# Laying the scratch copy of P out as one run of rows per batch, and issuing its transfers from SP

## The chip, the cores and the metric

The kernel runs on one core of a Trainium2 chip. The metric is the device time of one execution in microseconds (us). All numbers below are of one core, and "the profile" is one profiled execution of the kernel.

## What is computed

Eight batches of cross attention between 512 tokens `x` and 32 states per head feed one gated layer. The output is `(A * B) @ w_out`, with `A` and `B` the attention output times `w_a` and `w_b`.

```python
scores = scale * x @ state.T            # per batch (8) and head (8): 512 x 32
xread  = softmax(scores) @ state        # 512 x 64
scores2 = scale * state @ x.T
sread  = softmax(scores2) @ x           # 32 x 64
attn = concatenate([xread, sread], axis=2)   # 544 tokens a batch
X = attn.transpose(0, 2, 1, 3).reshape(8 * 544, 512)
out = (X @ w_a * (X @ w_b)) @ w_out     # w_a, w_b: 512 x 1536; w_out: 1536 x 512
```

The inputs are float32, and the products are made of high and low halves (`_h`, `_l`).

## The kernel before

`xread` is never formed. Since `xread @ w` is `softmax(scores) @ (state @ w)`, the kernel first makes P, the product of every head's states with that head's 64 rows of the weights, and then multiplies the attention weights `at_h`, `at_l` with P. The 1536 columns are taken in six chunks `c` of two column tiles `ft`. A head pair is `hp` (0 to 3), half a batch's heads are a group `g`, and four batches are a batch group `bg`.

- `load_w` and `conv_w` fetch a chunk's weights (64-bit words, `raw<-wl`, issued by SP) and split them on ACT and DVE into `wq`.
- `project` (L141 to L145) multiplies the split states `sd_h`, `sd_l` of four batches with `wq`. ACT copies the result from PSUM into `sw_st`, a tile with two buffers, once for each head `hh` of the pair, and after the second copy a transfer writes it to the scratch tensor `scr` in DRAM. In `scr` a batch's rows stand apart for each head.
- `Batch.load` (L269) reads one batch's part of P back into `p_raw` (two buffers), one transfer for each group `g`. All transfers into and out of `scr` are issued by ACT.
- `split` (L279, L65) turns `p_raw` into `p_h` and `p_l`, on ACT and on DVE or POOL. Four of the pieces are made by `direct` (L290 to L293) without `scr`.
- `layer1` (L379 to L387) multiplies P with the attention weights, and makes the gated product `g_h`, `g_l`. `layer2` (L402), two steps later, adds the output product into `acc`. Sums of a batch that is taken up again are kept in DRAM (`part`, L306 and L323).
- The attention itself (`x_raw`, `x_nat`, `s_p`, `at_h`, L178 to L240) and the last unit for the states' own tokens are spread among the steps.

The work is written as a list of 108 steps. A table (`VISITS`) gives the order of batches and chunks, and others give the step of each conversion. All projections and all first uses of P lie in the first half. A scheduler sets, when the kernel is built, one fixed order of instructions on each engine, and each engine then works through its own list, waiting where the next instruction's inputs or buffers aren't ready. Each transfer's completion is told through one of eight counters (`DMAHW0` to `DMAHW7`) that transfers of ACT and SP take in turn; a transfer that takes a counter again waits for the one before it on that counter.

Of the kernel before, what the change touches and what calls it, by code (L numbers as in the profile page):

```python
# [8 lines left out]
F32 = mybir.dt.float32  # L9
F32R = mybir.dt.float32r  # L10
# [6 lines left out]
B, H, S, NS, D = 8, 8, 512, 32, 64  # L17
DM, DFF = 512, 1536
P = 128
TOK = S + NS  # L20
NG = 2
NFT = DFF // P
NC = NFT // 2
# [25 lines left out]
def attn_moe(ctx, tc, xt, xn, sd, wl, w_out, out):  # L49
    nc = tc.nc  # L50

    const = ctx.enter_context(tc.tile_pool(name="const", bufs=1))
    proj = ctx.enter_context(tc.tile_pool(name="proj", bufs=2))
    att = ctx.enter_context(tc.tile_pool(name="att", bufs=2))
    mlp = ctx.enter_context(tc.tile_pool(name="mlp", bufs=2))
    dram = ctx.enter_context(tc.tile_pool(name="dram", bufs=1, space=bass.MemoryType.DRAM))
# [4 lines left out]
    def f32(ap):  # L61
        return ap.bitcast(F32)

    def minus(eng, out, in0, in1):
        eng.tensor_tensor(out=out, in0=in0, in1=in1, op=ALU.subtract)  # L65
# [40 lines left out]


    LO, HI, ALL = slice(0, D), slice(D, P), slice(0, P)
    sd_h = [proj.tile([P, 4, B * NS], F32R, name=f"sd_h{j}", bufs=1) for j in range(2)]
    sd_l = [proj.tile([P, 4, B * NS], F32R, name=f"sd_l{j}", bufs=1) for j in range(2)]  # L110

    def states():
        for j in range(2):
            raw = mlp.tile([P, 4, B * NS], F32, name="p_raw")
            nc.scalar.dma_start(out=raw, in_=sd[:, 4 * j:4 * j + 4])
            nc.scalar.copy(out=sd_h[j], in_=raw)
            minus(nc.gpsimd, sd_l[j], raw, f32(sd_h[j]))


    scr = [[dram.tile([H, 4 * NS, 512], F32, name=f"scr{c}_{g}") for g in range(2)] for c in range(NC)]  # L120
    w = {}

    def load_w(c, hp, place):
# [11 lines left out]
    def project(c, hp, bg, hh, psp, tag):  # L135
        if hh == 0:
            st[bg] = proj.tile([P, 2, 512], F32, name="sw_st")
        sw = st[bg]
        ps = psp.tile([P, 512], F32, name=tag)
        for k, s in enumerate((sd_h, sd_l)):  # L140
            nc.tensor.matmul(ps, lhsT=s[hp // 2][:, 2 * (hp % 2) + hh, bg * P:(bg + 1) * P], rhs=w[c, hp][:, hh],  # L141
                             start=(k == 0), stop=(k == 1))
        nc.scalar.copy(out=sw[:, hh], in_=ps)  # L143
        if hh:
            nc.scalar.dma_start(out=scr[c][bg][2 * hp:2 * hp + 2].rearrange("h n x -> n h x"), in_=sw)  # L145


    xst = const.tile([P, 4, B, NS], F32, name="xst")
# [15 lines left out]
    class Attention:  # L164
# [5 lines left out]
        def load(self):  # L170
            self.x = att.tile([P, 2, S + D], F32, name="x_raw", bufs=1)
            nc.sync.dma_start(out=self.x, in_=xt[self.b, self.g])
# [85 lines left out]
    class Batch:  # L258
        n, nk = S, NG
# [4 lines left out]

        def load(self, c):
            raw = self.raw[c] = mlp.tile([P, NG, 512], F32, name="p_raw")
            b = self.b
            for g in range(NG):
                nc.scalar.dma_start(out=raw[:, g],  # L269
                                    in_=scr[c][b // 4][4 * g:4 * g + 4, b % 4 * NS:(b % 4 + 1) * NS])  # L270

        def new_piece(self, c):
            self.pieces[c] = tuple(mlp.tile([P, NG, 512], F32R, name=n) for n in ("p_h", "p_l"))
# [8 lines left out]
        def direct(self, c, g):  # L282

            if g == 0:
                self.new_piece(c)
            ps = ps_ms.tile([P, 512], F32, name="ms")
            n = slice(self.b * NS, (self.b + 1) * NS)
            for i, s in enumerate((sd_h, sd_l)):
                for hq in range(4):
                    nc.tensor.matmul(ps[hq * NS:(hq + 1) * NS], lhsT=f32(s[g][:, hq, n]),  # L290
                                     rhs=f32(w[c, 2 * g + hq // 2][:, hq % 2]), start=(i == 0), stop=(i == 1))
            ph, pl = self.pieces[c]
            nc.scalar.copy(out=ph[:, g], in_=ps)  # L293
            minus(nc.vector, pl[:, g], ps, f32(ph[:, g]))
# [32 lines left out]
    class States:  # L327
        n, nk, begun = B * NS, 4, False
        pieces, raw = {}, {}
# [40 lines left out]
    def layer1(u, ft):  # L370
        res = []
        for ab in range(2):
            ps = ps_ab.tile([P, 512], F32, name="ab")
            m = 0
            for k in range(u.nk):
                xh, xl = u.rhs(k)
                wh, wlo = u.lhs(ft, k, ab)
                for a, b in ((wh, xh), (wh, xl), (wlo, xh)):
                    nc.tensor.matmul(ps[:, :u.n], lhsT=a, rhs=b, start=(m == 0), stop=(m == 3 * u.nk - 1))  # L379
                    m += 1  # L380
            res.append(ps)
        g = mlp.tile([P, 512], F32, name="a_sb")[:, :u.n]
        nc.scalar.copy(out=g, in_=res[0][:, :u.n])  # L383
        nc.vector.tensor_tensor(out=g, in0=res[1][:, :u.n], in1=g, op=ALU.mult)  # L384
        gh = mlp.tile([P, 512], F32R, name="g_h", bufs=LAG + 1)[:, :u.n]
        gl = mlp.tile([P, 512], F32R, name="g_l", bufs=LAG + 1)[:, :u.n]
        nc.scalar.copy(out=gh, in_=g)  # L387
        minus(nc.vector, gl, g, f32(gh))
        return gh, gl
# [31 lines left out]
    def mms(where, n, c, hp, bg):  # L421
        for hh in range(2):
            at(where, n, project, c, hp, bg, hh, *((ps_acc, "acc") if n < 0 else (ps_ms, "ms")))
# [28 lines left out]
    def conv0(hp):  # L452
# [3 lines left out]
    a0, a1, a2 = [[atts[b, g] for g in range(2)] for b in range(3)]  # L456
    done[0] = -1
    begin += [a0[0].load, next_load, states, lambda: new_a(0),
              lambda: conv0(0), a0[0].scores, a0[0].soft, a0[1].load, lambda: conv0(1), a0[0].norm,
              a0[1].scores, a0[0].nat, lambda: units[0].direct(0, 0), a0[0].back]  # L460
# [39 lines left out]
    for v, (u, cs) in enumerate(VISITS):  # L500
        s = starts[v]
# [7 lines left out]
        for i, c in enumerate(cs):  # L509
            n = s + 2 * i  # L510
# [5 lines left out]
            t = max(n - 6, (CONV[c][3] + 1 if c else 0) + u // 4)  # L516
# [9 lines left out]
    for n, (u, ft, first, last, final) in enumerate(steps):  # L526
        for f in front[n]:
            f()
        g = layer1(u, ft)
# [50 lines left out]
```

## Time and profile before

| | |
|---|---|
| median of 3 runs | 810.42 us (809.29 to 811.74) |
| profiled execution: its time, its span | 809.78 us, 807.9 us |
| busy in the span: PE, DVE, ACT, POOL | 736.5, 504.7, 372.5, 130.1 us |
| mean granted TensorE clock | 0.966 |
| transfers of P: stores of 512 KB, loads of 256 KB | 48, 88 |

PE (TensorE) is the busiest engine. Busy times are sums over the whole run, and the first 450 us are another regime than the rest: projections, conversions and attention run beside the two layers there. A row of the chain view reads: start, length, what the last-ended work was then doing or waiting for. A row of the timeline has the start, the length, the engine, line, operation and tiles, and, in brackets, how long the engine sat idle before it and what ended that. ACTq and SPq are the engines' queues of transfer issues. PEld is the loading of weights, which overlaps PE.

### The profile page before, as it was taken

Reading aid. Unit: us, or ns where it says so; the run is one execution under the profiler, and the core shown is the slowest. Engines: PE = TensorE matmul, PEld = TensorE weight load, DVE = VectorE, ACT = ScalarE, POOL = GpSimd, SP = SyncE. Lnnn points to the kernel's source line nnn. Section 1 sums busy time; section 2 is a strip of 40 time slices with the busy share of each in tenths; the row PEclk is TensorE's granted clock in tenths of the full one; section 3 lists DMA queues with packets and bytes.
Section 4 is the critical chain, followed back from the end, with each engine's and each line's share of the span. In section 5 each row is a group of like instructions: output and inputs, shape, how many; then the busy total and the mean of one; then the engine's idle time right before and its main releaser. Section 6 shows DMA issues by size and latency. Waiting matters only on the chain.

```text
span 807.9 us, 9570 instructions
## 1 busy us (share of the span) xinstructions
PE 736.5 (91%) x3384; PEld 555.2 (69%) x3384; DVE 504.7 (62%) x885; ACT 372.5 (46%) x686; POOL 130.1 (16%) x100
## 2 busy tenths in 40 slices
PE   1668879898998999998889999999999999999997
PEld 0345545573765768886667677777788888888886
DVE  5977851866996675685269573654435953596422
ACT  4546644735654455665444333343334633453222
POOL 3213110001222031010022241322110010100100
PEclk9989779999998999999999999999999999999999
DMA  8567854586366536556657772413013521241002
GB/s 315 194 232 264 285 189 156 174 295 239 125 229 230 197 139 240 193 183 222 232 199 255 236 236 77 148 39 130 30 51 101 188 75 53 66 145 52 1 1 79
DMA packets 52560, 131.17 MB, mean 162 GB/s; under 512 B 3872, under 2 KB 3872, under 8 KB 52512
## 3 DMA queue, kind: packets, MB, share of 16 engines
q1 hardware_dynamic: 27552, 81.28, 29.7%
q10 hardware_dynamic: 24960, 49.29, 17.0%
q8 instruction: 26, 0.43, 0.2%
q14 instruction: 22, 0.18, 0.1%
HBM read 84.93 MB, written 45.61 MB: 162 GB/s over the span
## 4 chain that ended last, share of the span: by engine, by line
PE 64%; DMA 15%; DVE 12%; ACT 5%; issue 2%; ACTq 1%; POOL 0%; DVEq 0%; POOLq 0%
PE ab L379 29%; PE acc L402 27%; DMA scr<-sw_st 8%; DMA p_raw<-scr 4%; PE ms L141 3%; PE ms L231 2%; DMA x_nat<-xn 2%; DVE t L92 1%; DVE wq L104 1%; DVE t L99 1%; DVE t L97 1%; ACT sw_st L143 1%; PE ms L178 1%; DMA raw<-wl 1%; PE ms L290 1%
## 5 line engine op out<-in xcount | busy, mean ns | idle before, releaser
L402 PE MATMUL acc<-wo,g_h 128*128 128x512 f32 x816 | 240.7, 399 | 4.3 <-DVE stg L318 4.3
L402 PEld LDWEIGHTS acc<-wo,g_h 128*128 128x128 f32 x816 | 153.3, 190 | 42.6 <-DVE stg L318 6.8
L384 DVE TENSOR_TENSOR a_sb<-ab,a_sb 128x512 f32<-128x512 f32 (+1 forms) x108 | 71.1, 658 | 173.6 <-PE ab L379 137.9
L379 PE MATMUL ab<-at_h,p_h 128*128 128x512 f32 x384 | 158.8, 416 | 11.3 <-ACT a_sb L383 7.3
L379 PE MATMUL ab<-at_h,p_l 128*128 128x512 f32 x384 | 153.4, 403 | 3.5 <-DVE p_l L65 3.5
L379 PE MATMUL ab<-at_l,p_h 128*128 128x512 f32 x384 | 154.8, 403 | 0.9 <-POOL at_l L65 0.9
L402 PE MATMUL acc<-wo,g_l 128*128 128x512 f32 x408 | 143.2, 399 | 0.0
L65 POOL TENSOR_TENSOR p_l<-p_raw,p_h 128x512 fp32r<-128x512 f32 x44 | 65.0, 1477 | 428.5 <-ACT p_h L279 385.9
L65 DVE TENSOR_TENSOR g_l<-a_sb,g_h 128x512 fp32r<-128x512 f32 (+1 forms) x108 | 91.0, 843 | 32.8 <-ACT g_h L387 31.0
L383 ACT COPY a_sb<-ab 128x512 f32<-128x512 f32 (+1 forms) x108 | 60.7, 562 | 101.6 <-PE ab L379 92.7
L387 ACT CAST g_h<-a_sb 128x512 fp32r<-128x512 f32 (+1 forms) x108 | 64.4, 596 | 86.9 <-DVE a_sb L384 86.3
L379 PEld LDWEIGHTS ab<-at_h,p_h 128*128 128x128 f32 x384 | 73.5, 193 | 39.7 <-ACT a_sb L383 10.3
L402 PEld LDWEIGHTS acc<-wo,g_l 128*128 128x128 f32 x408 | 77.4, 190 | 19.8 <-DVE g_l L65 1.0
L379 PEld LDWEIGHTS ab<-at_h,p_l 128*128 128x128 f32 x384 | 73.8, 193 | 23.1 <-DVE p_l L65 4.4
L379 PEld LDWEIGHTS ab<-at_l,p_h 128*128 128x128 f32 x384 | 74.4, 194 | 18.9 <-POOL at_l L65 2.2
L143 ACT COPY sw_st<-ms 128x512 f32<-128x512 f32 x88 | 50.8, 587 | 57.2 <-PE ms L141 22.1
L279 ACT CAST p_h<-p_raw 128x512 fp32r<-128x512 f32 x88 | 50.8, 619 | 49.9 <-PE ab L379 31.4
L141 PE MATMUL ms<-wq,sd_h 128*128 128x512 f32 x88 | 37.9, 431 | 10.3 <-ACT sw_st L143 9.5
L90 DVE TENSOR_SCALAR t<-t 128x512 int32<-128x512 int32 x60 | 28.2, 472 | 28.1 <-ACT t L89 27.6
L95 ACT CAST wq<-t 64x512 fp32r<-64x512 f32 (+1 forms) x64 | 39.4, 620 | 12.7 <-PE ms L290 4.9
L65 POOL TENSOR_TENSOR s_p<-s_p,m 128x512 f32<-128x512 f32 x16 | 18.3, 1146 | 113.1 <-DVE m L193 113.1
L141 PE MATMUL ms<-wq,sd_l 128*128 128x512 f32 x88 | 36.3, 413 | 0.0
(89 smaller groups left out, 816.2 us busy)
## 6 DMA issues: line engine op xcount, KB each, us to landing
scr<-sw_st ACTq DMA_DIRECT2D x48, 512.0 KB
p_raw<-scr ACTq DMA_DIRECT2D x88, 256.0 KB
raw<-wl SPq DMA_DIRECT2D x23, 512.0 KB
x_raw<-xt SPq DMA_DIRECT2D x16, 576.0 KB
part<-stg SPq DMA_DIRECT2D x18, 512.0 KB
stg<-part SPq DMA_DIRECT2D x18, 512.0 KB
out<-stg SPq DMA_DIRECT2D x34, 256.0 KB
x_nat<-xn SPq DMA_DIRECT2D x16, 512.0 KB
```

The costliest lines, as they stand in the source:

```text
L65: eng.tensor_tensor(out=out, in0=in0, in1=in1, op=ALU.subtract)
L90: nc.vector.tensor_scalar(out=t2, in0=t1, scalar1=3, scalar2=0x7FFFF000, op0=ALU.logical_shift_left, op1=ALU.bitwise_and)
L95: nc.scalar.copy(out=o, in_=f32(t2[rows]))
L141: nc.tensor.matmul(ps, lhsT=s[hp // 2][:, 2 * (hp % 2) + hh, bg * P:(bg + 1) * P], rhs=w[c, hp][:, hh], start=(k == 0), stop=(k == 1))
L143: nc.scalar.copy(out=sw[:, hh], in_=ps)
L231: nc.tensor.matmul(ps[hp * D:(hp + 1) * D, :P], lhsT=self.a2[:, sb, hp * D:(hp + 1) * D], rhs=self.xn[:, sb, hp * P:(hp + 1) * P], start=( ...
L279: nc.scalar.copy(out=ph[:, g], in_=self.raw[c][:, g])
L379: nc.tensor.matmul(ps[:, :u.n], lhsT=a, rhs=b, start=(m == 0), stop=(m == 3 * u.nk - 1))
L383: nc.scalar.copy(out=g, in_=res[0][:, :u.n])
L384: nc.vector.tensor_tensor(out=g, in0=res[1][:, :u.n], in1=g, op=ALU.mult)
L387: nc.scalar.copy(out=gh, in_=g)
L402: nc.tensor.matmul(u.acc[i], lhsT=l[:, ts], rhs=wo[ft][:, r], start=(first and k == 0), stop=(last and k == 2))
```

## The change

`scr` gets the shape group, batch of four, head of four, state, so that one batch's 128 rows of a group stand in one run. To let a store keep whole rows, the states' columns in `sd_h` and `sd_l` are put in the order state, batch (`states`, which now makes four copies of half the size with a reordering access), so that the projection's output rows come out in that order too. A store of 512 KB becomes two of 256 KB, one for each head. A load of both groups becomes one transfer of 512 KB. Both are issued by SP (`nc.sync`) instead of ACT (`nc.scalar`). `direct` reads its 32 columns of the states with a step of four.

```diff
-    sd_h = [proj.tile([P, 4, B * NS], F32R, name=f"sd_h{j}", bufs=1) for j in range(2)]
+    sd_h = [proj.tile([P, 4, 2, P], F32R, name=f"sd_h{j}", bufs=1) for j in range(2)]
...
-            nc.scalar.copy(out=sd_h[j], in_=raw)
-            minus(nc.gpsimd, sd_l[j], raw, f32(sd_h[j]))
+            for bg in range(2):
+                h, l = (t[j][:, :, bg].rearrange("p h (n b) -> p h b n", b=4) for t in (sd_h, sd_l))
+                r = raw[:, :, bg * P:(bg + 1) * P].rearrange("p h (b n) -> p h b n", b=4)
+                nc.scalar.copy(out=h, in_=r)
+                minus(nc.gpsimd, l, r, f32(h))
...
-    scr = [[dram.tile([H, 4 * NS, 512], F32, name=f"scr{c}_{g}") for g in range(2)] for c in range(NC)]
+    scr = [[dram.tile([NG, 4, 4, NS, 512], F32, name=f"scr{c}_{g}") for g in range(2)] for c in range(NC)]
...
         if hh:
-            nc.scalar.dma_start(out=scr[c][bg][2 * hp:2 * hp + 2].rearrange("h n x -> n h x"), in_=sw)
+            h = 2 * (hp % 2)
+            for i in range(2):
+                nc.sync.dma_start(out=scr[c][bg][hp // 2, :, h + i].rearrange("b n x -> n b x"), in_=sw[:, i])
...
-            for g in range(NG):
-                nc.scalar.dma_start(out=raw[:, g],
-                                    in_=scr[c][b // 4][4 * g:4 * g + 4, b % 4 * NS:(b % 4 + 1) * NS])
+            nc.sync.dma_start(out=raw, in_=scr[c][self.b // 4][:, self.b % 4].rearrange("g h n x -> (h n) g x"))
...
-                    nc.tensor.matmul(ps[hq * NS:(hq + 1) * NS], lhsT=f32(s[g][:, hq, n]),
+                    nc.tensor.matmul(ps[hq * NS:(hq + 1) * NS], lhsT=f32(s[g][:, hq, self.b // 4, self.b % 4::4]),
```

The orders below are those fixed when the kernels are built; lines are each kernel's own (L143 before is L148 after, L145 is L152, L269 is L274). The first place is ACT in the third chunk's projections, about 168 to 178 us into the profile of before. Before:

```order
L387 CAST g_h<-a_sb 128x512 [waits DVE_49]
L269 DMA p_raw<-scr_0_91 128x1x512 [waits DMAHW7_49,DMAHW4_49]
L269 DMA p_raw<-scr_0_91 128x1x512 [waits DMAHW0_49,Pool_49]
L143 COPY sw_st<-ms 128x512 [waits PE_49]
L383 COPY a_sb<-ab 128x512 [waits PE_49]
L145 DMA scr_1_92<-sw_st 128x2x512 [waits DMAHW1_49,Activation_49]
L143 COPY sw_st<-ms 128x512 [waits PE_49]
L387 CAST g_h<-a_sb 128x512 [waits DVE_49]
```

and after, on ACT at the same place:

```order
L390 CAST g_h<-a_sb 128x512 [waits DVE_49]
L148 COPY sw_st<-ms 128x512 [waits PE_49]
L148 COPY sw_st<-ms 128x512 [waits DMAHW1_49,DMAHW4_49,PE_49,Activation_49]
L386 COPY a_sb<-ab 128x512 [waits PE_49]
L390 CAST g_h<-a_sb 128x512 [waits DVE_49]
```

The loads and the store are gone from ACT's list. What stays is the copy's own wait for the buffer, now for two counters, since a buffer is left by two stores.

The second place is SP where the fifth chunk ends and the sixth begins, about 330 to 375 us. Before, SP has only weights there:

```order
L78 DMA raw<-wl 128x2x512 [waits DMAHW7_49,DVE_49]
L78 DMA raw<-w_out 128x1024 [waits DMAHW3_49,DVE_49,Activation_49]
L78 DMA raw<-w_out 128x1024 [waits DMAHW3_49,DMAHW5_49,DVE_49,Activation_49]
L78 DMA raw<-wl 128x1024 [waits DMAHW7_49,DVE_49]
L78 DMA raw<-wl 128x1024 [waits DMAHW1_49,DMAHW5_49,DVE_49,Activation_49]
```

and after, a part of the same stretch:

```order
L152 DMA scr_1_96<-sw_st 32x4x512 [waits DMAHW5_49,Activation_49]
L78 DMA raw<-w_out 128x1024 [waits DMAHW6_49,DMAHW2_49,DVE_49]
L152 DMA scr_1_96<-sw_st 32x4x512 [waits DMAHW7_49,Activation_49]
L78 DMA raw<-wl 128x1024 [waits DMAHW0_49,DVE_49]
L274 DMA p_raw<-scr_1_96 128x2x512 [waits DMAHW5_49,DMAHW7_49,DMAHW1_49,Pool_49]
L152 DMA scr_0_97<-sw_st 32x4x512 [waits Activation_49]
L152 DMA scr_0_97<-sw_st 32x4x512 [waits DMAHW3_49,Activation_49]
L78 DMA raw<-wl 128x1024 [waits DMAHW6_49,DMAHW4_49,DVE_49]
L152 DMA scr_1_98<-sw_st 32x4x512 [waits Activation_49]
L274 DMA p_raw<-scr_0_95 128x2x512 [waits DMAHW1_49,DVE_49,Pool_49]
```

The two halves of a store stand between loads of weights that wait for DVE, and the load of a piece, which waits for its stores to land, stands ahead of the next chunk's stores.

More of the change, by code (lines that the diff above doesn't have):

```diff
@@ L108, in attn_moe @@
     LO, HI, ALL = slice(0, D), slice(D, P), slice(0, P)
-    sd_h = [proj.tile([P, 4, B * NS], F32R, name=f"sd_h{j}", bufs=1) for j in range(2)]
-    sd_l = [proj.tile([P, 4, B * NS], F32R, name=f"sd_l{j}", bufs=1) for j in range(2)]
+    sd_h = [proj.tile([P, 4, 2, P], F32R, name=f"sd_h{j}", bufs=1) for j in range(2)]
+    sd_l = [proj.tile([P, 4, 2, P], F32R, name=f"sd_l{j}", bufs=1) for j in range(2)]
     def states():
@@ L140, in project @@
         for k, s in enumerate((sd_h, sd_l)):
-            nc.tensor.matmul(ps, lhsT=s[hp // 2][:, 2 * (hp % 2) + hh, bg * P:(bg + 1) * P], rhs=w[c, hp][:, hh],
+            nc.tensor.matmul(ps, lhsT=s[hp // 2][:, 2 * (hp % 2) + hh, bg], rhs=w[c, hp][:, hh],
                              start=(k == 0), stop=(k == 1))
@@ L266, in load @@
             raw = self.raw[c] = mlp.tile([P, NG, 512], F32, name="p_raw")
-            b = self.b
-            for g in range(NG):
-                nc.scalar.dma_start(out=raw[:, g],
-                                    in_=scr[c][b // 4][4 * g:4 * g + 4, b % 4 * NS:(b % 4 + 1) * NS])
+            nc.sync.dma_start(out=raw, in_=scr[c][self.b // 4][:, self.b % 4].rearrange("g h n x -> (h n) g x"))
         def new_piece(self, c):
@@ L286, in direct @@
             ps = ps_ms.tile([P, 512], F32, name="ms")
-            n = slice(self.b * NS, (self.b + 1) * NS)
             for i, s in enumerate((sd_h, sd_l)):
                 for hq in range(4):
-                    nc.tensor.matmul(ps[hq * NS:(hq + 1) * NS], lhsT=f32(s[g][:, hq, n]),
+                    nc.tensor.matmul(ps[hq * NS:(hq + 1) * NS], lhsT=f32(s[g][:, hq, self.b // 4, self.b % 4::4]),
                                      rhs=f32(w[c, 2 * g + hq // 2][:, hq % 2]), start=(i == 0), stop=(i == 1))
```

## Prediction

> **What bounds the kernel now.** I read the page first, for the whole and for PE:
>
> ```profile
> span 807.9 us, 9570 instructions
> PE 736.5 (91%) x3384; PEld 555.2 (69%) x3384; DVE 504.7 (62%) x885; ACT 372.5 (46%) x686; POOL 130.1 (16%) x100
> PE ab L379 29%; PE acc L402 27%; DMA scr<-sw_st 8%; DMA p_raw<-scr 4%; PE ms L141 3%; PE ms L231 2%; DMA x_nat<-xn 2%; DVE t L92 1%; DVE wq L104 1%; DVE t L99 1%; DVE t L97 1%; ACT sw_st L143 1%; PE ms L178 1%; DMA raw<-wl 1%; PE ms L290 1%
> ```
>
> PE is busy 91% of the span, so 71 us of it are idle. In the chain of waits the transfers of P hold 8% and 4%, some 97 us. That is a ceiling and not a gain: behind a chain there is always a second one. To place it, the stages (busy us of each engine, then granted clock, DMA share, GB/s):
>
> ```profile
> 28.00:62.00 34.00, 25.44 (x126) 14.46 (x127) 29.39 (x60) 16.48 (x32) 7.02 (x7) 0.85 0.68 225
> 160.00:196.00 36.00, 31.71 (x130) 22.67 (x130) 22.59 (x42) 14.86 (x29) 1.48 (x1) 0.93 0.76 278
> 200.00:250.00 50.00, 46.25 (x223) 34.88 (x222) 48.57 (x89) 29.90 (x56) 13.93 (x11) 1.00 0.54 192
> 354.00:410.00 56.00, 48.41 (x199) 37.51 (x198) 25.18 (x39) 25.27 (x47) 4.53 (x4) 0.97 0.67 231
> 450.00:808.00 358.00, 353.14 (x1697) 285.16 (x1695) 191.17 (x319) 135.06 (x249) 53.92 (x38) 1.00 0.28 93
> ```
>
> From 450 us on PE is full and DMA is at 0.28: loads of P are hidden there, and I cost that stage at nothing. What the change can move lies in three stages, 28 to 62, 160 to 196 and 354 to 410 us. Between them, at 200 to 250, DVE is busy 48.57 of 50 us: time won ahead of it is in part waited out there. The pieces of the chain in these stages (start, length):
>
> ```profile
> 41.17 9.57 DMA scr<-sw_st
> 129.96 2.86 DMA scr<-sw_st
> 164.73 8.25 DMA scr<-sw_st
> 174.81 7.66 DMA scr<-sw_st
> 355.14 5.21 DMA p_raw<-scr
> 361.55 9.09 DMA scr<-sw_st
> 381.13 15.01 DMA scr<-sw_st
> 400.86 8.26 DMA p_raw<-scr
> ```
>
> The same 512 KB store takes 2.86 us when nothing is in its way, and 7.7 to 15 us here. Next, who sat idle for it: ACT, by all its waits and at six places, and then PE at the same places.
>
> ```profile
> ACT sw_st L143 <- DMA scr<-sw_st: 21.5, 8, 6.0
> ACT p_h L279 <- DMA p_raw<-scr: 18.4, 6, 7.0
> 51.98 0.59 ACT L383 COPY a_sb<-ab 128x512 f32<-128x512 f32 x1 [6.20 <-DMA p_raw<-scr]
> 174.19 0.59 ACT L143 COPY sw_st<-ms 128x512 f32<-128x512 f32 x1 [5.54 <-issue]
> 182.54 0.59 ACT L143 COPY sw_st<-ms 128x512 f32<-128x512 f32 x1 [5.41 <-DMA scr<-sw_st]
> 370.72 1.08 ACT L143 COPY sw_st<-ms 128x512 f32<-128x512 f32 x2 [4.49 <-DMA scr<-sw_st]
> 396.23 1.07 ACT L143 COPY sw_st<-ms 128x512 f32<-128x512 f32 x2 [6.04 <-DMA scr<-sw_st]
> 409.14 0.62 ACT L279 CAST p_h<-p_raw 128x512 fp32r<-128x512 f32 x1 [7.04 <-DMA p_raw<-scr]
> 52.62 0.80 PE L379 MATMUL ab<-at_h,p_h 128*128 128x512 f32 x1 [3.28 <-ACT a_sb L383]
> 183.18 0.51 PE L141 MATMUL ms<-wq,sd_h 128*128 128x512 f32 x1 [1.84 <-ACT sw_st L143]
> 194.49 0.50 PE L379 MATMUL ab<-at_h,p_h 128*128 128x512 f32 x1 [1.85 <-ACT p_h L293]
> 371.36 0.50 PE L141 MATMUL ms<-wq,sd_h 128*128 128x512 f32 x1 [3.19 <-ACT sw_st L143]
> 396.86 0.50 PE L141 MATMUL ms<-wq,sd_h 128*128 128x512 f32 x1 [2.45 <-ACT sw_st L143]
> 410.29 0.50 PE L379 MATMUL ab<-at_h,p_h 128*128 128x512 f32 x1 [2.23 <-ACT a_sb L383]
> ```
>
> Two kinds of stall show. At 51.98, at 174.19 and before 194.49 ACT had nothing of its own to wait for: a load of P in its list waited for a store to land, and everything behind the load stood. At the others a copy waits for its `sw_st` buffer, or a split for its load. PE loses less than ACT, 14.8 us in these six rows, because it has other matmuls queued.
>
> Last, the transfers themselves:
>
> ```profile
> DMA packets 52560, 131.17 MB, mean 162 GB/s; under 512 B 3872, under 2 KB 3872, under 8 KB 52512
> q10 hardware_dynamic: 24960, 49.29, 17.0%
> ```
>
> q10 is ACT's queue. Its data packets are rows: 88 x 128 + 48 x 256 + 2 x 128 (the states) = 23808. The other 1152 are the small ones that tell of completion. If the 48 stores and 2 loads of states leave 16 each, one for each DMA engine, that is 800, and 352 are left for 88 loads: 4 each. So a load of P runs on 4 of the 16 DMA engines, and on those four everything behind it waits.
>
> **The change, part by part.**
>
> Loads leave ACT (first kind of stall). All three waits move to SP, on which no engine's arithmetic waits. PE's idle time there is 3.28 and 1.85 us; at 174.19 it has other work. Gain 5.1 us; at the least 0, if the next input is as late as the issue was.
>
> Loads change shape. The Trainium skill, "DMA: Bandwidth & Descriptors", section "Why a DMA increments its semaphore by 16 and not by 1", says that a transfer runs on the largest number of engines up to 16 that divides the slowest dimension of both sides; by it the old loads, with 4 heads outermost, get 4, which the count bears out, and the new ones, with 128 rows, get 16. No run here shows the new load yet. From rows: it carries 512 KB like the store that took 2.86, against 5.21 for 256 KB now, so 2.9 to 5.2 us a piece, and I take 3.5, nearer the row of its size. The split at 409.14 waited 7.04 of a load's 8.26 us. With the load at 5 us amid its neighbours, the wait shrinks by 3.3, and PE's 2.23 by the same share, 1.0 us.
>
> Stores land sooner (second kind). Above the 2.86 of an unhindered store the rows at 174.81, 361.55 and 381.13 have 4.8, 6.2 and 12.1 us. Part of that is loads on four engines ahead of the store, part is plain traffic, since DMA shares of 0.67 and 0.76 remain whoever issues. I take half: 2.4, 3.1 and 6.0 off the waits of 5.41, 4.49 and 6.04, which leaves 3.0, 1.4 and 0 of them; in proportion PE's 1.84, 3.19 and 2.45 shrink by 0.8, 2.2 and 2.45. Gain 5.5 us, between 0 and 7.5.
>
> The clock. The three stages lost 0.15 x 34 + 0.07 x 36 + 0.03 x 56 = 9.3 us to a granted clock under 1. PE idling less may bring a third back: 3 us, between 0 and 5.
>
> Costs. `states` makes four copies in place of two, and `direct` reads columns with a step:
>
> ```profile
> L116 ACT CAST sd_h<-p_raw 128x1024 fp32r<-128x1024 f32 x2 | 2.1, 1040 | 3.6 <-DMA p_raw<-sd 3.6
> L290 PEld LDWEIGHTS ms<-wq,sd_l 128*32 128x32 f32 x64 | 2.2, 119 | 5.8 <-issue 5.8
> ```
>
> Two casts of half the size at the 0.62 of a 128x512 one (row 409.14) are 0.2 us longer than one of 1.04, twice, on ACT while DVE's conversions lead: 0.2 us taken, 0 to 1. The stepped columns might double a load of 119 ns; over 128 that is 15 us at most, beside matmuls that last longer, so 0 taken. The two issues per store cost SP, not a working engine, some 0.4 us. A first half of a piece can no longer be loaded before the other is stored, but no split of these stages waits on the first half alone for long: 0.
>
> SP's own waits are the serious cost, since P now stands behind them (waits of SP's queue: us, times, longest):
>
> ```profile
> SPq L78 <- DVE wq L104: 273.8, 29, 65.5
> SPq L306 <- DMA part<-stg: 22.5, 9, 4.7
> ```
>
> Today nothing urgent is behind them: weights come early, and sums have slack. After the change stores stand behind both. The second sort is 2.5 us each; about five have a store of P behind them, and a store that is late by that is mostly covered by the other `sw_st` buffer. I take 2 us, and leave the first sort to a rival.
>
> Sum: 5.1 + 1.0 + 5.5 + 3 - 0.2 - 2 = 12.4 us less than the profiled execution's 809.8 (span 807.9 and 1.9 around it). The median of 810.4 stands 0.6 above that execution, so 798.0; I forecast 797.
>
> **The rivals.**
>
> Slower: SP holds the stores back. A load of weights that waits for DVE now stands between the halves of a store. A mean wait of the first SP row is 273.8 / 29 = 9.4 us. A step of the two layers is 24 matmuls, 5.8 us:
>
> ```profile
> 482.46 2.99 PE ab L379 x12
> 485.45 2.80 PE acc L402 x12
> ```
>
> A step with a conversion makes two stores, one for each batch group, and there are two buffers, so a store that is late by 9.4 us stalls ACT's copy, and PE after it, by some 3.6 us. Three to four such places use up the gain of 12.4, six give 798 + 22 = 820, and one wait as long as the longest, 65.5 us, would do it alone: 813 to 835. For it: the new order on SP shows such neighbours for each chunk. Against it: the order follows when things are expected to be ready, and on ACT stores already stood behind waits of the same size. The point of decision is whether DVE frees `raw` later than ACT finishes the copy beside it.
>
> Same: the queue does not matter. The Trainium skill, same page, section "Issuing engines are not separate DMA queues", says that issuing from several engines only saves the time to issue. In this kernel that would mean the waits for landing bind whoever issues: SP waits for a store in place of ACT, the buffers come free no sooner, and the time is 808 to 812. The rows speak against it in part: ACT stood 6.20 and 5.54 us for an issue alone.
>
> Much faster: the chain is the right measure. If the five long stores in the chain rows (49.6 us) came down to 2.86 each, 35 us would be gained there alone: 770 to 778. Against it: DVE's 48.57 of 50 us, and PE's idle rows, 14.8 us against 66 in the eight chain rows.
>
> **How the numbers follow.** Forecast (785 to 807) 0.56; slower 0.24; same 0.12; much faster 0.08. The range leaves about one in ten on each side: 774 to 822. What a measurement can tell from no change is 0.3%, 2.4 us. Faster than that: 0.56 + 0.08 and a little of the others' edges, 0.65; within: 0.11; slower: 0.24.
>
> **What would show it.** Right: the small packets show 16 for every load in place of 4; ACT's waits for P (21.5 and 18.4) halve; the first kind of stall is absent from ACT; the store rows in the chain fall under 6 us; from 450 us on nothing changes but the start. Wrong: SP rows with stores of P behind `raw` loads, ACT's `sw_st` waits above 21.5 us, or PE idle as long for other inputs, DVE's above all.

## The result, and the profile after

The changed kernel takes 784.1 us (median of four runs, 781.05 to 787.78) against 810.77 us for the kernel before (809.29 to 811.74): a ratio of 0.9675, 95% interval 0.9625 to 0.9724. That is 26.7 us less, where 12.4 us less were worked out. The profiled execution took 785.89 us, with a span of 784.1 us. The head of the profile's page, with the lines on packets, on SP's and ACT's queues (q1, q10), on the chain and on the issues of P:

```profile
span 784.1 us, 9701 instructions
PE 724.5 (92%) x3384; PEld 550.3 (70%) x3384; DVE 509.8 (65%) x885; ACT 374.0 (48%) x688; POOL 133.2 (17%) x102
...
DMA packets 53681, 131.18 MB, mean 167 GB/s; under 512 B 4992, under 2 KB 4992, under 8 KB 53632
...
q1 hardware_dynamic: 53344, 129.52, 48.1%
q10 hardware_dynamic: 288, 1.05, 0.4%
...
PE ab L382 30%; PE acc L405 29%; PE ms L146 3%; DMA scr<-sw_st 3%; DVE wq L104 3%; DVE t L92 3%; DVE t L99 3%; DMA raw<-wl 2%; DVE t L97 2%; PE ms L238 1%; DMA raw<-w_out 1%; DMA p_raw<-scr 1%; DVE a_sb L387 1%; PE ms L185 1%; DVE t L90 1%
...
scr<-sw_st SPq DMA_DIRECT2D x96, 256.0 KB, 3.7
p_raw<-scr SPq DMA_DIRECT2D x44, 512.0 KB, 3.8
```

In the chain the transfers of P fell from 8% and 4% to 3% and 1%, and single lines of the conversions of weights on DVE (`t`, `wq`) are now, at 3% each, as large as the stores; together these conversions hold 12%. The small packets rose from 3872 to 4992: 48 more stores at 16 are 768, and 44 loads at 16 in place of 88 at 4 are 352 more. The sum is 1120, the whole difference, so a load of P now runs on 16 engines.

From the span and PE's busy time a split follows that the prediction did not make. Before, 736.5 us busy and 71.4 idle; after, 724.5 and 59.6. So 11.8 us are idle time saved, and 12.0 us are the same 3384 matmuls running shorter. The mean granted clocks agree: 0.966 of 807.9 us leaves 27.5 us without clock, 0.980 of 784.1 us leaves 15.7, which is 11.8 us less. The windows show where (busy us of each engine, then granted clock, DMA share, GB/s):

```profile
28.00:62.00 34.00, 26.23 (x127) 13.82 (x126) 30.83 (x61) 17.58 (x33) 8.99 (x8) 0.85 0.78 258
62.00:160.00 98.00, 81.76 (x388) 53.76 (x387) 63.59 (x119) 57.70 (x109) 15.53 (x12) 0.91 0.59 207
160.00:196.00 36.00, 32.25 (x152) 21.74 (x151) 25.80 (x48) 19.09 (x37) 2.75 (x2) 1.00 0.85 308
250.00:300.00 50.00, 48.38 (x229) 36.76 (x230) 39.02 (x68) 26.42 (x50) 8.81 (x7) 1.00 0.54 179
354.00:410.00 56.00, 54.23 (x243) 41.10 (x242) 37.38 (x64) 31.73 (x60) 10.22 (x8) 1.00 0.78 270
```

In the window 160 to 196 PE does 152 matmuls where it did 130, though its busy time grew by only 0.5 us; the clock there went from 0.93 to 1.00. At 354 to 410 us it does 243 in place of 199. The window at 28 to 62 is as it was, at a clock of 0.85 and with 127 matmuls. The windows are fixed in time, so the later ones hold later work. Two windows of the kernel before that the prediction didn't show:

```profile
62.00:160.00 98.00, 81.37 (x384) 52.04 (x382) 60.47 (x118) 57.21 (x108) 14.96 (x13) 0.89 0.61 213
250.00:300.00 50.00, 44.59 (x196) 33.42 (x196) 34.51 (x60) 24.75 (x45) 8.84 (x7) 0.93 0.52 183
```

At 250 to 300 us the clock went from 0.93 to 1.00 and the matmuls from 196 to 229; at 62 to 160 us both hardly moved. By 450 us PE has done 1787 matmuls in place of 1689, and 33 of these 98 come from the window at 250 to 300 us, which was not among the three stages of the prediction.

The waits of ACT and of SP's queue, of PE, and the transfers of P that are left in the chain:

```profile
ACT t L89 <- DMA raw<-wl: 16.8, 8, 5.1
ACT sw_st L148 <- DMA scr<-sw_st: 15.2, 7, 3.5
ACT p_h L283 <- DMA p_raw<-scr: 10.4, 5, 3.5
SPq L274 <- DVE p_l L65: 196.9, 30, 16.0
SPq L274 <- DMA scr<-sw_st: 18.8, 8, 3.8
PE ab L382 <- ACT a_sb L386: 4.3, 2, 3.1
```

```profile
41.18 5.05 DMA scr<-sw_st
46.29 4.23 DMA p_raw<-scr
129.43 2.43 DMA scr<-sw_st
182.97 5.49 DMA scr<-sw_st
188.52 4.09 DMA p_raw<-scr
354.44 5.97 DMA scr<-sw_st
377.44 5.01 DMA scr<-sw_st
```

ACT's two waits for P fell from 21.5 and 18.4 to 15.2 and 10.4 us, and the stores of 7.7 to 15 us in the chain are now 5.0 to 6.0. SP stands 196.9 us in front of loads of P whose buffer isn't free yet, with weights and stores queued behind. Still ACT's waits for the weights `wl` grew little, from 14.4 to 16.8 us.

### The profile page after: what moved, and what is told of

Read it like the earlier page. It is cut to its first block, busy times and chain, and to the rows that moved or that the text cites. A ratio compares the mean times of both kernels' runs of the same rounds, so it can differ in the third digit from the quotient of the medians.

```text
span 784.1 us, 9701 instructions
## 1 busy us (share of the span) xinstructions
PE 724.5 (92%) x3384; PEld 550.3 (70%) x3384; DVE 509.8 (65%) x885; ACT 374.0 (48%) x688; POOL 133.2 (17%) x102
## 2 busy tenths in 40 slices
DMA packets 53681, 131.18 MB, mean 167 GB/s; under 512 B 4992, under 2 KB 4992, under 8 KB 53632
## 4 chain that ended last, share of the span: by engine, by line
PE 66%; DVE 18%; DMA 9%; issue 3%; ACT 2%; POOL 1%; SPq 0%; DVEq 0%; ACTq 0%
PE ab L382 30%; PE acc L405 29%; PE ms L146 3%; DMA scr<-sw_st 3%; DVE wq L104 3%; DVE t L92 3%; DVE t L99 3%; DMA raw<-wl 2%; DVE t L97 2%; PE ms L238 1%; DMA raw<-w_out 1%; DMA p_raw<-scr 1%; DVE a_sb L387 1%; PE ms L185 1%; DVE t L90 1%
## 5 line engine op out<-in xcount | busy, mean ns | idle before, releaser
L65 POOL TENSOR_TENSOR p_l<-p_raw,p_h 128x512 fp32r<-128x512 f32 x44 | 63.0, 1433 | 412.3 <-ACT p_h L283 340.1
L382 PEld LDWEIGHTS ab<-at_h,p_l 128*128 128x128 f32 x384 | 73.0, 191 | 20.8 <-DVE p_l L65 4.2
L382 PEld LDWEIGHTS ab<-at_l,p_h 128*128 128x128 f32 x384 | 73.1, 190 | 18.8 <-POOL at_l L65 3.6
L148 ACT COPY sw_st<-ms 128x512 f32<-128x512 f32 x88 | 50.4, 589 | 33.2 <-PE ms L146 17.0
L90 DVE TENSOR_SCALAR t<-t 128x512 int32<-128x512 int32 x60 | 30.4, 507 | 24.9 <-ACT t L89 24.3
L95 ACT CAST wq<-t 64x512 fp32r<-64x512 f32 (+1 forms) x64 | 39.4, 621 | 11.4 <-PE ms L293 4.9
L65 DVE TENSOR_TENSOR p_l<-p_raw,p_h 128x512 fp32r<-128x512 f32 x44 | 36.5, 829 | 8.8 <-ACT p_h L283 8.8
```

The source lines that it names most:

```text
L90: nc.vector.tensor_scalar(out=t2, in0=t1, scalar1=3, scalar2=0x7FFFF000, op0=ALU.logical_shift_left, op1=ALU.bitwise_and)
L95: nc.scalar.copy(out=o, in_=f32(t2[rows]))
```

## The experiments

The change has two parts that can be separated: the queue (ACT or SP) and the shape of the loads (4 engines or 16, "narrow" and "wide" below). Each ratio is against runs of the kernel before on the same chip, with its 95% interval.

### Each part alone

e1_act keeps the new layout and loads, and gives them back to ACT:

```diff
-                nc.sync.dma_start(out=scr[c][bg][hp // 2, :, h + i].rearrange("b n x -> n b x"), in_=sw[:, i])
+                nc.scalar.dma_start(out=scr[c][bg][hp // 2, :, h + i].rearrange("b n x -> n b x"), in_=sw[:, i])
-            nc.sync.dma_start(out=raw, in_=scr[c][self.b // 4][:, self.b % 4].rearrange("g h n x -> (h n) g x"))
+            nc.scalar.dma_start(out=raw, in_=scr[c][self.b // 4][:, self.b % 4].rearrange("g h n x -> (h n) g x"))
```

> The changed kernel with ACT issuing all stores and loads of P again; layout, one load of 512 KB and two stores of 256 KB stay. If the queue makes the gain (ACT stood behind loads that wait for stores), nearly all of it is lost: 803 to 812 us, and ACT again idles over 12 us behind loads of P. If the width of the loads makes it (a load on all DMA engines in place of 4), it stays: 784 to 792 us. If each does half: 794 to 802 us.

e2_old_sp is the kernel before, with only the queue changed:

```diff
-            nc.scalar.dma_start(out=scr[c][bg][2 * hp:2 * hp + 2].rearrange("h n x -> n h x"), in_=sw)
+            nc.sync.dma_start(out=scr[c][bg][2 * hp:2 * hp + 2].rearrange("h n x -> n h x"), in_=sw)
-                nc.scalar.dma_start(out=raw[:, g],
+                nc.sync.dma_start(out=raw[:, g],
```

> The kernel before with its 48 stores and 88 loads of P, in the old layout, issued by SP: the queue alone. If the queue makes the gain: 784 to 792 us. If the width of the loads makes it: 805 to 815 us. If each does half: 794 to 802 us. If SP's waits for DVE hold back P without the faster loads: over 815 us.

Measured: e1_act 781.85 us, ratio 0.9633 (0.9577 to 0.9689); e2_old_sp 828.36 us, ratio 1.0204 (1.0144 to 1.0265). So the layout on ACT gives the whole gain, and the queue alone costs some 17 us. That ACT's freed list makes the gain is borne out neither with wide loads nor with narrow ones. Waits of e2_old_sp on ACT and of SP's queue and PE:

```profile
ACT t L89 <- DMA raw<-wl: 29.2, 7, 7.9
ACT p_h L279 <- DMA p_raw<-scr: 28.0, 7, 9.7
SPq L269 <- DVE p_l L65: 179.0, 26, 16.0
PE ms L141 <- ACT sw_st L143: 16.6, 7, 6.6
```

ACT waits 29.2 us for weights (14.4 before) and PE 16.6 us for the copies out of PSUM (9.5 before). The row of SP's own waits is as large here (179.0) as in the changed kernel (196.9), which is fast: that row alone does not tell whether SP's waits hurt.

### The width of the loads, all else in place

e5b_two cuts the changed kernel's load into two wide ones. e5_four does the same, but leaves a spare row in `scr` after every 32, so that the source can't be seen as 128 even rows:

```diff
-    scr = [[dram.tile([NG, 4, 4, NS, 512], F32, name=f"scr{c}_{g}") for g in range(2)] for c in range(NC)]
+    scr = [[dram.tile([NG, 4, 4, NS + 1, 512], F32, name=f"scr{c}_{g}") for g in range(2)] for c in range(NC)]
...
-            nc.sync.dma_start(out=raw, in_=scr[c][self.b // 4][:, self.b % 4].rearrange("g h n x -> (h n) g x"))
+            for g in range(NG):
+                nc.sync.dma_start(out=raw[:, g], in_=scr[c][self.b // 4][g, self.b % 4, :, :NS])
```

The first two lines are of e5_four alone (and its store writes `:NS`). The traces of both have the same instructions in the same order on every engine.

> As the run with two loads of 256 KB, but scr has one spare row after every 32, so that the rows of a load no longer stand in one run and it goes out with 4 heads outermost, on 4 DMA engines as before (small packets 16 - 4 = 12 fewer for each of 88 loads). The order of instructions on every engine is that of its partner. If the width makes the gain: 800 to 812 us. If the queue makes it: 782 to 790 us. If each does half: 792 to 800 us.

> The changed kernel with a piece loaded by two transfers of 256 KB, one for each group, in place of one of 512 KB. Every theory: within 0.5% of the changed kernel, 780 to 788 us; if the single transfer itself matters (issue time on SP, 44 completions more), 786 to 792 us. It is the partner of the next run.

e11_two_engines puts the spare row after every 64 rows:

```diff
+    scr = [[dram.tile([NG, 4, 2, 2 * NS + 1, 512], F32, name=f"scr{c}_{g}") for g in range(2)] for c in range(NC)]
```

> As the run with four-engine loads on SP, with the spare row after every 64 rows: 2 rows of blocks outermost, so 2 DMA engines a load, with the same order of instructions. A second 256 KB load on four engines lands 2.1 us after the first, so on two it should take 4.2. If the narrow loads' time on their few engines makes the loss (44 us from 16 to 4): the loss grows to 100 to 180 us, 880 to 960 us. If the loss were something of the spare rows and not of the width: about 828 us.

Measured: e5b_two 783.73 us, ratio 0.964 (0.9572 to 0.9708); e5_four 827.88 us, 1.0201 (1.0144 to 1.0257); e11_two_engines 927.33 us, 1.1437 (1.1399 to 1.1475). Two wide loads are as good as one. e5_four lies above every range expected for it: the width costs more on SP's queue than the whole gain of the change. The packet lines of the three pages, in this order, say on how many engines a load runs:

```profile
DMA packets 54385, 131.18 MB, mean 168 GB/s; under 512 B 5696, under 2 KB 5696, under 8 KB 54336
```

```profile
DMA packets 53329, 131.18 MB, mean 159 GB/s; under 512 B 4640, under 2 KB 4640, under 8 KB 53280
```

```profile
DMA packets 53153, 131.18 MB, mean 142 GB/s; under 512 B 4464, under 2 KB 4464, under 8 KB 53104
```

Small packets: 5696 - 4640 = 1056 = 88 x 12, and 5696 - 4464 = 1232 = 88 x 14. With 16 a load in the first, the others have 4 and 2. The counts bear out the rule of the Trainium skill, "DMA: Bandwidth & Descriptors", section "Why a DMA increments its semaphore by 16 and not by 1", for 2, 4 and 16. What each width costs on SP's queue: 784, 828 and 927 us for the same bytes in the same order. From e5_four to e5b_two PE's idle time falls from 92.7 to 58.6 us and its busy time from 733.8 to 724.4, so 34.1 us are waits and 9.4 us are matmuls that run shorter. Transfers in the chain of e5_four from 250 to 345 us, and then three of ACT's waits there, show who is late:

```profile
251.94 9.24 DMA raw<-wl
268.47 6.43 DMA raw<-wl
...
287.22 6.91 DMA raw<-wl
303.59 8.82 DMA raw<-w_out
334.48 9.93 DMA raw<-wl
```

```profile
ACT p_h L284 <- DMA p_raw<-scr: 30.9, 7, 8.5
ACT sw_st L148 <- DMA scr<-sw_st: 26.8, 8, 6.2
ACT t L89 <- DMA raw<-wl: 24.8, 8, 7.5
```

The chain's are loads of weights, which didn't change. Those named `wl` take 6.4 to 9.9 us here, and 4.6 to 6.1 us in the chain of e5b_two. But the weights are not the largest loss: in e5b_two the three waits of ACT are 7.3, 12.4 and 20.8 us, so the wait for the loads of P themselves grew most (by 23.6 us), then that for the stores (14.4), and that for `wl` least (4.0). So the stores, cut into the same halves in both runs, are late because of the loads' width.

### Whose queue the narrow loads are in

Two variants of e5_four: e6_four_loads_act issues the narrow loads from ACT (stores on SP), e10_four_stores_act the stores from ACT (narrow loads on SP).

```diff
-                nc.sync.dma_start(out=raw[:, g], in_=scr[c][self.b // 4][g, self.b % 4, :, :NS])
+                nc.scalar.dma_start(out=raw[:, g], in_=scr[c][self.b // 4][g, self.b % 4, :, :NS])
```

> The four-engine loads (scr with a spare row after every 32, two loads of 256 KB a piece) go back to ACT's queue, the stores stay on SP. If narrow loads hurt most what stands behind them in the same queue, on the same four DMA engines, the weights, tokens and stores of SP are free of them: 803 to 815 us, against 828 with all on SP. If the queue plays no part and only the four engines' load does: 824 to 832 us. The width's own cost stays either way, so not under 800.

> The other way round: four-engine loads on SP, stores on ACT. If the 17 us between four-engine loads on SP and on ACT come from stores that SP issues late, behind its waits for DVE, they come back: 808 to 815 us. If they come from weights and tokens that land late behind narrow loads in SP's queue: 820 to 832 us.

Measured: e6_four_loads_act 812.71 us, ratio 1.0015 (0.9989 to 1.004); e10_four_stores_act 824.71 us, 1.0189 (1.0139 to 1.0238). Away from SP's queue the narrow loads cost what they cost in the kernel before: of the 44 us between e5_four and e5b_two, 15 go with the queue and 29 stay. Taking the stores out of the queue instead changes little, so those 15 us are not paid for late stores. ACT's waits, of e6_four_loads_act and then of e10_four_stores_act:

```profile
ACT t L89 <- DMA raw<-wl: 14.9, 7, 4.7
```

```profile
ACT t L89 <- DMA raw<-wl: 36.3, 7, 8.1
ACT sw_st L148 <- DMA scr<-sw_st: 7.0, 3, 3.0
```

With the stores on ACT the wait for the buffer of stores is down to 7.0 us (26.8 in e5_four), but the wait for weights is 36.3 us (24.8 there; e10_four_stores_act's profiled execution was its longest, 831.3 us). PE's wait for the tokens `x_raw`, also issued by SP, is 16.1 us in e5_four, 14.6 in e10_four_stores_act, and 6.4 in e6_four_loads_act. So weights and tokens behind the narrow loads are what moves with the 15 us; that they make the whole of them is not shown.

What stays on ACT's queue shows in the time from issue to landing. The page has no such medians where loads are narrow; counted from the completion counters in the traces (a transfer has landed with the last of its updates), they are, in us over the whole execution:

| | load of P, 256 KB | store, 256 KB | `raw<-wl` | `x_raw<-xt` |
|---|---|---|---|---|
| e5b_two: wide loads on SP | 2.9 | 3.3 | 5.2 | 5.8 |
| e5_four: narrow loads on SP | 7.2 | 5.2 | 6.9 | 7.5 |
| e6_four_loads_act: narrow loads on ACT | 7.5 | 4.4 | 6.4 | 6.8 |

A narrow load itself takes more than twice as long, whoever issues it. The transfers beside it land later too, and a queue of their own gives them back only a part of that.

### Wide loads in the old layout

e12_old_by_head leaves the layout and ACT's queue of the kernel before, and cuts each load into four, one for each head's 32 rows (64 KB), which run on 16 engines:

```diff
-                nc.scalar.dma_start(out=raw[:, g],
-                                    in_=scr[c][b // 4][4 * g:4 * g + 4, b % 4 * NS:(b % 4 + 1) * NS])
+                for h in range(4):
+                    nc.scalar.dma_start(out=raw[h * NS:(h + 1) * NS, g],
+                                        in_=scr[c][b // 4][4 * g + h, b % 4 * NS:(b % 4 + 1) * NS])
```

> The kernel before, in its old layout and all on ACT, with each load of 4 heads cut into one transfer for each head: 32 rows, 64 KB, 352 loads in place of 88. If the width is what counts and not the run of rows, each is spread over 16 DMA engines: 780 to 795 us, the upper end if 264 more issues at some 0.5 us cost ACT time. If the layout counts by itself: 805 to 815 us.

e13_by_head_sp issues these loads from SP (`nc.sync`), the stores still from ACT.

> e12_old_by_head with its 352 cut loads (64 KB each, all 16 DMA engines) issued by SP in place of ACT; the stores stay on ACT, the scratch stays in the layout of before. Theory A, that what e12_old_by_head lost against e1_act (800.8 against 781.9 us) is the time in which ACT stood still while it issued eight loads a piece (88.0 us of idle before a_sb on p_raw): 782 to 792 us, and that idle is gone from ACT. Rival B, that 64 KB transfers in the old layout cost by themselves, whoever issues them: 797 to 804 us. Rival C, that SP, held by its loads in the same way, now lets the weights and token blocks behind them come late: 800 to 820 us, with more of ACT's waits for raw<-wl than the 7.0 us of e1_act.

Measured: e12_old_by_head 800.78 us, ratio 0.9873 (0.9838 to 0.9909); e13_by_head_sp 794.06 us, 0.9813 (0.9769 to 0.9857). The first lies between the two ranges expected for it. The wide loads gain here too, 11.3 and 15.9 us, against 29.5 us in the new layout on ACT. What e12_old_by_head pays stands in ACT's waits:

```profile
ACT a_sb L384 <- DMA p_raw<-scr: 88.0, 18, 8.3
```

Eight issues a piece hold ACT's list 18 times; in the trace at least 295 of the 352 wait for the completion counter of an earlier transfer. Which of the two took more of the 88.0 us was not measured apart. In e13_by_head_sp this row is 2.4 us in one place, and these stand in its stead, on ACT and in SP's queue:

```profile
ACT t L89 <- DMA raw<-wl: 26.0, 9, 6.4
SPq L270 <- DMA scr<-sw_st: 66.0, 18, 14.1
```

In the profiled executions PE's idle time falls from 71.5 to 62.1 us with the busy time the same (727.6 and 727.9). But the intervals of the two ratios overlap, and theory A's 782 to 792 us was missed by 2: that ACT's waits were part of the loss is likely and not shown. The 10 us that still lie between e13_by_head_sp and the changed kernel are not explained. The weights' 26.0 us (16.8 in the changed kernel) and SP's 66.0 us in front of loads whose stores haven't landed (18.8 there) speak for SP's list being held in the same way, which was rival C's sign, yet the time is below its range.

### The start

The changed kernel's first product of `layer2` is later than before. e7_host has the states put in the new order where the inputs are laid out, so that ACT and POOL copy them without a step, and e7_act is that with all transfers of P on ACT.

```diff
-            for bg in range(2):
-                h, l = (t[j][:, :, bg].rearrange("p h (n b) -> p h b n", b=4) for t in (sd_h, sd_l))
-                r = raw[:, :, bg * P:(bg + 1) * P].rearrange("p h (b n) -> p h b n", b=4)
-                nc.scalar.copy(out=h, in_=r)
-                minus(nc.gpsimd, l, r, f32(h))
+            v = raw.rearrange("p h (g x) -> p h g x", g=2)
+            nc.scalar.copy(out=sd_h[j], in_=v)
+            minus(nc.gpsimd, sd_l[j], v, f32(sd_h[j]))
```

> The changed kernel with the states laid out in the order state, batch before the launch, so that ACT and POOL copy them whole and in a row again (two casts and two subtractions in place of four and four with a step). The reordering casts took 1122 ns each, four of them, where two of 1040 stood; POOL 1615 ns in place of 2564 for double the size. If that sits at the start's path: 1.5 to 2.5 us less than the changed kernel, 781 to 783 us. If DVE's conversions hide it: 784 us.

> The same with all stores and loads of P issued by ACT, which with wide loads was 781.9 us. If the start's 2 us and the queue's 2 us add up: 779 to 780.5 us, the fastest version here. If neither is real: 782 to 784 us.

Measured: e7_host 785.91 us, ratio 0.9672 (0.9642 to 0.9703); e7_act 782.09 us, 0.9621 (0.959 to 0.9652). The same matmul in the timelines of before, after and e7_host:

```profile
57.05 2.02 PE L402 MATMUL acc<-wo,g_h 128*128 128x512 f32 x8
```

```profile
59.42 2.02 PE L405 MATMUL acc<-wo,g_h 128*128 128x512 f32 x8
```

```profile
57.71 2.02 PE L403 MATMUL acc<-wo,g_h 128*128 128x512 f32 x8
```

The 2.4 us at the start are there, and 1.7 of them go when the copies have no step, but nothing of that shows at the end. No version is shown to beat the changed kernel: e1_act and e7_act have the lowest medians, with intervals that overlap its own.

## Why the prediction was right, and where its sum was not

The direction was right, the place in part, and the reason for a good part of the gain was not. The time of 784.1 us lies in the whole range, 774 to 822, but just under the band of 785 to 807 that the forecast was given, and the gain is over twice the sum. That the sum came out on the right side was also luck: its term for the queue was worth nothing, and the wide loads that the same change brought made up for it. By its steps:

- **What bounds the kernel.** Held in part: the gain was made before 450 us, and the windows at 160 and 354 us gained 22 and 44 matmuls. But the one at 250 to 300 us, which the prediction left out, gained 33, and the one at 28 to 62 us gained nothing: PE's 3.28 us at 52.62 are there after the change too, as 3.06 us, by the timeline of ACT and PE:

```profile
50.55 1.14 ACT L283 CAST p_h<-p_raw 128x512 fp32r<-128x512 f32 x2 [2.40 <-DMA p_raw<-scr]
52.89 0.51 PE L382 MATMUL ab<-at_h,p_h 128*128 128x512 f32 x1 [3.06 <-ACT a_sb L386]
```

  ACT now waits there for the load itself, with the split, where before a load in its list held a copy.
- **"Loads leave ACT", 5.1 us: the step that failed.** It was read from ACT standing 6.20 us before a copy because a load was stuck in its list. The stall is gone from ACT, but e1_act, with the loads back in ACT's list, is as fast, and e2_old_sp is 17 us slower than before. The term was near its lower bound of 0: at 52 us the input was as late as the issue had been.
- **"Loads change shape" 1.0 and "stores land sooner" 5.5 us: right mechanism, too small a term.** Their cause is one, the width, and it is worth 30 us on ACT's queue (before against e1_act, the layout's other edits included) and 44 us on SP's (e5_four against e5b_two). The new load took 4.1 and 4.2 us in the chain, between the 3.5 taken for it and the 5 that its wait was worked out with. ACT's waits for P, which were to halve, fell by 29% (stores) and 43% (loads). PE's waits for the copy into `sw_st`, by its waits of before and its line of groups after:

```profile
PE ms L141 <- ACT sw_st L143: 9.5, 6, 3.2
```

```profile
L146 PE MATMUL ms<-wq,sd_h 128*128 128x512 f32 x88 | 37.1, 421 | 4.7 <-ACT sw_st L148 2.1
```

  They fell by some 7.4 us, at the upper bound of 7.5 taken for the stores. That weights and tokens, too, land sooner beside wide loads was in no term. In the changed kernel it can't be seen in ACT's waits, as P is now in the weights' queue (14.4 us for `wl` before, 16.8 after); in e1_act, with P on ACT, they are 7.0 us.
- **"The clock", 3 us and 5 at most: the largest miss.** PE's busy time fell by 12.0 us for the same matmuls. I had counted three stages and 9.3 us, where the mean clock leaves 27.5 us over the whole run; a low clock also stood at 62 to 160 us (0.89, then 0.91) and at 250 to 300 us (0.93, then 1.00). The idle terms came to 9.4 us with the costs taken off, and 11.8 us were measured, though divided otherwise among their causes. So of the 11.4 us that the profiled execution gained beyond the sum, 9.0 are this term.
- **Costs.** The 0.2 us for the states (at most 1) was low: the start is 2.4 us later. Nothing of it is left at the end. SP's own waits, 2 us: the changed kernel's median is 2.2 us above e1_act's, which the intervals can't tell from nothing.
- **The rival "slower"** is not what happened, but its mechanism exists: narrow loads in SP's queue give 828 us in e2_old_sp and e5_four, inside its 813 to 835. What was late in e2_old_sp was the weights (29.2 us), the tokens (13.7 us of PE's waits, 6.4 before) and the loads of P (28.0 us) rather than the stores it named (14.4 us, 21.5 before), and narrow loads rather than waits for DVE decided it.
- **The rival "same"** was half right: with wide loads the queue does not matter. With narrow ones it does, 812.7 against 827.9 us (e1_act against the changed kernel, 781.9 and 784.1, is the first pair; this is the second). The sentence of the Trainium skill behind it ("DMA: Bandwidth & Descriptors", section "Issuing engines are not separate DMA queues") agrees with the first pair of runs and not with the second, where the weights behind the narrow loads landed after 6.9 us in the same queue and 6.4 in another, the tokens after 7.5 and 6.8.
- **"Much faster"** was not reached; the chain's 35 us overstated, as DVE's conversions of weights came up behind the stores (1% a line in the chain before, 2 to 3% for most after).

## What to carry to other kernels

Count the small completion packets of a transfer before arguing about queues: a load that ran on 4 of 16 engines took 7.2 us in place of 2.9, in either queue, and what ran beside it landed later too, most of all in its own queue. Here it was enough to lay the scratch out so that the slowest dimension of both sides is a multiple of 16. Two transfers of 256 KB did as well as one of 512 KB; eight of 64 KB, in the old layout, did not, and held the list of the engine that issued them (88.0 us of ACT's). When PE has idle time to lose, estimate the clock with it, over all stages in which it is under 1.

## What the runs showed that I had not expected

The granted clock went with PE's idle time. Mean clocks of the runs: 0.962 to 0.972 for the kernel before (beside e13_by_head_sp), 0.976 to 0.987 for those with wide loads of 256 or 512 KB, 0.958 to 0.963 for e2_old_sp's and e5_four's profiled executions, and 0.909 in that of e11_two_engines, where PE idles 178.4 of 927.0 us. That one causes the other is not shown; no run changed PE's idling alone.

Casts that write with a step of four were dear on ACT: the states' casts in the new kernel take as long as casts of twice the size before (1040 ns each for 128x1024).

```profile
L120 ACT CAST sd_h<-p_raw 128x512 fp32r<-128x512 f32 x4 | 4.1, 1125 | 3.8 <-DMA p_raw<-sd 3.8
```

An unstepped cast of 128x512 takes 619 ns. And the issue of one 256 KB store from SP takes 524 ns (median) where one of 512 KB from ACT took 366. The engine is not the reason, since the same store takes 526 ns on ACT in e1_act. A narrow load of 256 KB takes 527 ns to issue in e5_four, a wide one 382 in e5b_two.
